# Running every main product of a transformer kernel in 64-row tile mode

## The chip, the cores and the metric

The kernel runs on one core of one Trainium2 chip. The metric is the device time of one execution in microseconds (us), as a median over several executions. Every call on the chip also ran the kernel before, so that each kernel is compared with it on the same chip.

The engines are named as in the profile: PE is TensorE's matmul, PEld its weight load, DVE VectorE, ACT ScalarE, POOL GpSimd, SP SyncE (here it only issues DMAs). PSUM is the memory that PE writes its products to; the program lays it out as eight banks of 128 rows by 512 f32 columns, so that a product of 512 columns takes a whole bank.

## The reference

The reference runs two kinds of layers, A and B, twice each, over 2048 tokens of width 448. Inputs and weights are bf16.

```python
def A(x, wqkv, wo):        # 16 heads of 28; each token sees 8 keys, 2 apart, behind it
    q, k, v = split(x @ wqkv)
    attn = softmax(mask(q . k[s - 2*w]) * 28 ** -0.5)      # w = 0..7
    return (attn . v) @ wo                                  # 448 -> 448
def B(x, w_gate, w_up, w_down):
    return ((x @ w_gate) * (x @ w_up)) @ w_down             # 448 -> 1792 -> 448

x = x + A(layernorm(x)); x = x + B(layernorm(x))
x = x + A(layernorm(x)); x = x + B(layernorm(x))
```

## The kernel before

A small scheduler inside the program takes all operations with their dependences and estimated lengths, and orders them for each engine. It interleaves the attention of one part of the tokens with the feed-forward of another. Some of its settings are the "knobs" of the change: `A_CAP` limits the PSUM banks that attention may hold, `HOLD_A` and `HOLD_BA` say how long an operation of another PE mode waits before it interrupts the main products.

The contraction over 448 is three chunks of 128 rows and one of 64. The program uses PE as one array of 128 rows, or as two tiles of 64 rows that work at the same time (the 64-row mode; in the trace below the two halves start 3 ns apart). The kernel before uses the full array for the 128-row chunks, and pairs the two 64-row remainders of gate and up (or of K and Q, or of two V blocks) in the 64-row mode: six full products and one pair, seven slots in all, for two outputs.

```python
def paired(tag, li, j, first, second, tdeps, prio):
    ...
    first["last"] = full(first, 0, True, ...)       # three 128-row products of gate, mode "F"
    first["last"] = full(first, 1, True)            # three of up, mode "F"
    ...
    tails([(first, False), (second, True)])         # 64-row remainders, both halves at once, mode "R64"
    second["last"] = full(second, 0, False)         # mode "F" again
    second["last"] = full(second, 1, False)

def y_block(li, B, prio):                           # output projection of one block of 128 tokens
    bk = Banks(1)
    ...
    for hc in range(4):
        ins.append((lambda E, hc=hc: E.matmul(ps[:, bk[0], 0:D], oT[:, hc, lo:hi], wo_g[:, hc, :], start=hc == 0, stop=hc == 3), ...))
    sc.add("pe", ins, 4 * pe_cols(D), deps=nd + WO, mode="F", acquire=bk, prio=prio)

# down projection, in b_chunk: 14 full products of 128 rows per block, mode "F"
# gate and up weights: WG and WU [128, 3, F] over all rows, and the remainders in WT [128, F]
```

Attention's own products are in two more modes: scores use tiles of 28 rows ("R32"), values tiles of 32 columns ("C32").

The softmax here doesn't subtract the row's maximum and nothing guards it: scores larger than these inputs give would overflow.

## Time and profile before

| | before |
|---|---|
| median (lowest to highest), 3 runs | 419.69 us (419.61 to 420.73) |
| span of the profiled run | 418.8 us |
| PE busy | 96% of the span |
| DVE, ACT busy | 65%, 50% |
| mean granted clock, profiled run | 0.988 |

The page of the profile gives busy time by engine, busy tenths in 40 slices (PEclk is the granted clock in tenths), and the chain of work that ended last.

```profile
span 418.8 us, 7454 instructions
...
PE 400.5 (96%) x3047; PEld 174.3 (42%) x3092; DVE 273.7 (65%) x553; ACT 210.0 (50%) x341; POOL 28.1 (7%) x40
...
PE   5896999999999999999999999999999999999997
...
PEclk8699999999999999999999999999999999999999
...
PE 88%; DVE 5%; ACT 3%; DMA 2%; issue 1%
```

PE is the limit: after the first tenth of the span it is busy all the time and it makes up most of the chain. The windows of 100 us each say the same (window, length, then busy us of PE, PEld, DVE, ACT and POOL, granted clock, DMA share, GB/s).

```profile
100.00:200.00 100.00, 98.89 (x756) 43.76 (x766) 73.22 (x151) 47.70 (x78) 0.00 (x0) 1.00 0.11 22
200.00:300.00 100.00, 98.73 (x756) 42.79 (x766) 68.58 (x138) 50.38 (x81) 0.00 (x0) 1.00 0.14 25
300.00:400.00 100.00, 98.89 (x665) 41.41 (x672) 57.00 (x105) 42.51 (x70) 0.00 (x0) 1.00 0.10 22
```

"Busy" does not mean "at its peak", because the ends of matmuls are modelled. The groups of the page show it (operation, shapes and count, then busy us, mean ns of one).

```profile
L540 PE MATMUL ps<-xnTb,WU 128*128 128x512 bf16 x330 | 89.8, 379 | 0.8 <-issue 0.3
...
L552 PE MATMUL ps<-xnTb,WT 64*128 64x512 bf16 x224 | 33.8, 381 | 0.0
...
L512 DVE TENSOR_SCALAR xn_sb<-x_sb,mv,rstd 128x512 bf16<-128x512 bf16 x64 | 22.6, 405 | 2.4 <-ACT rstd L506 2.4
```

A product of 512 columns is recorded with 379 ns, but the next one starts after 216. So I read the starts. This is the timeline of PE from 203.8 us (start, length, what, count).

```profile
203.61 0.38 PE L540 MATMUL ps<-xnTb,WG 128*128 128x512 bf16 x1
203.92 0.39 PE L680 MATMUL ps<-qk 28*128 28x120 bf16 x16
204.47 0.59 PE L540 MATMUL ps<-xnTb,WU 128*128 128x512 bf16 x2 [0.16 <-issue]
204.99 0.60 PE L552 MATMUL ps<-xnTb,WT 64*128 64x512 bf16 x4
205.53 0.82 PE L540 MATMUL ps<-xnTb,WG 128*128 128x512 bf16 x3
```

In 2 us the mode changes four times. The single starts of that stretch, in ns, taken from the same trace:

```
204466 full product (128 rows, 512 columns)
204682 full product              + 216   same mode
204994 64-row product, half 1    + 312   mode change: 96 more
204997 64-row product, half 2    +   3   both halves run together
205219 64-row product, half 1    + 222   next pair
205531 full product              + 312   mode change: 96 more than 216
```

DMA issues at the start of the program, as the page lists them (count, KB each, median us from issue to landing):

```profile
WD<-in_B_w_down_dram POOLq DMA_DIRECT2D x1, 1568.0 KB, 14.5
WG<-in_B_w_gate_dram POOLq DMA_DIRECT2D x3, 448.0 KB, 4.7
WU<-in_B_w_up_dram POOLq DMA_DIRECT2D x3, 448.0 KB, 7.9
...
xnTb<-xn_sb SPq DMA_TRANSPOSE x32, 2.5
```

### The profile page before, as it was taken

To read this page: it belongs to the slowest core of one execution; us is meant where nothing else is said; L and a number is where in the kernel's file an instruction comes from. 1 tells how busy PE (TensorE), PEld (TensorE's weight loads), DVE (VectorE), ACT (ScalarE), POOL (GpSimd) and SP (SyncE) were. 2 spreads that over 40 slices of the span, in tenths; PEclk is the share of its full clock that TensorE was granted. 3 is DMA by queue.
4 is the path that set the end of the run, shared out by engine and by line. 5 is a ranking of instruction groups with operands and counts; after the bars stand their busy time and mean duration, and the time that the engine had idled before them with its cause. 6 is when DMAs were issued, how large, how long until landed. Compare 5 with 4: busy or idle time off the path is not lost.

```text
span 418.8 us, 7454 instructions
## 1 busy us (share of the span) xinstructions
PE 400.5 (96%) x3047; PEld 174.3 (42%) x3092; DVE 273.7 (65%) x553; ACT 210.0 (50%) x341; POOL 28.1 (7%) x40
## 2 busy tenths in 40 slices
PE   5896999999999999999999999999999999999997
PEld 3333334444434444444343443434444443444343
DVE  5757897557788647876558875787367846843342
ACT  4579976653456256461555337655255625421320
POOL 3714530000000000000000000000000000000000
PEclk8699999999999999999999999999999999999999
DMA  8793123000003001120100401022100210040001
GB/s 280 224 299 69 37 42 52 13 2 2 13 14 75 2 2 26 26 53 0 27 0 2 77 0 27 2 50 38 34 0 2 50 35 13 0 63 33 0 2 44
DMA packets 37217, 18.08 MB, mean 43 GB/s; under 512 B 31136, under 2 KB 36272, under 8 KB 37184
## 3 DMA queue, kind: packets, MB, share of 16 engines
q1 hardware_dynamic: 34880, 11.02, 12.4%
q0 software_dynamic: 1152, 5.22, 4.1%
q10 hardware_dynamic: 1152, 1.38, 0.9%
q8 instruction: 24, 0.39, 0.4%
q14 instruction: 9, 0.07, 0.1%
HBM read 8.43 MB, written 1.84 MB: 25 GB/s over the span
## 4 chain that ended last, share of the span: by engine, by line
PE 88%; DVE 5%; ACT 3%; DMA 2%; issue 1%
PE ps L540 47%; PE ps L797 20%; PE ps L552 10%; PE ps L742 5%; PE ps L711 2%; PE ps L680 2%; ACT E_sb L687 1%; DVE qk L614 1%; PE ps L579 1%; DMA x_sb<-in_A_x_dram 1%; DVE st L501 1%; DVE oT L728 1%; DMA xnTb<-xn_sb 1%; DVE E_sb L693 1%; DVE x_sb L747 1%
## 5 line engine op out<-in xcount | busy, mean ns | idle before, releaser
L785 DVE TENSOR_TENSOR hT<-g_sb,ps 128x512 bf16<-128x512 bf16 x112 | 74.5, 684 | 32.5 <-ACT g_sb L782 25.2
L782 ACT ACTIVATE g_sb<-ps 128x512 bf16<-128x512 f32 x112 | 64.7, 599 | 58.2 <-PE ps L552 48.2
L540 PE MATMUL ps<-xnTb,WU 128*128 128x512 bf16 x330 | 89.8, 379 | 0.8 <-issue 0.3
L797 PE MATMUL ps<-WD,hT 128*128 128x448 bf16 x448 | 89.4, 353 | 0.0
L540 PE MATMUL ps<-xnTb,WG 128*128 128x512 bf16 x310 | 85.6, 380 | 2.5 <-issue 2.2
L687 ACT ACTIVATE E_sb<-ps 128x960 bf16<-128x960 f32 (+1 forms) x72 | 63.5, 925 | 40.9 <-PE ps L680 40.8
L747 DVE TENSOR_TENSOR x_sb<-x_sb,ps 128x448 bf16<-128x448 bf16 x64 | 39.5, 617 | 42.2 <-PE ps L797 32.6
L693 DVE TENSOR_TENSOR E_sb<-E_sb,MK 128x960 bf16<-128x960 bf16 (+1 forms) x64 | 41.6, 651 | 37.1 <-ACT E_sb L687 36.8
L797 PEld LDWEIGHTS ps<-WD,hT 128*128 128x128 bf16 x448 | 43.0, 98 | 41.0 <-issue 0.4
L540 PE MATMUL ps<-xnTa,WQK 128*128 128x512 bf16 x179 | 46.4, 392 | 3.5 <-ACT WQK L462 1.6
L540 PEld LDWEIGHTS ps<-xnTb,WU 128*128 128x128 bf16 x336 | 32.5, 98 | 38.3
L540 PEld LDWEIGHTS ps<-xnTb,WG 128*128 128x128 bf16 x336 | 27.7, 98 | 48.2 <-issue 24.0
L614 ACT ACTIVATE qk<-ps 128x1024 bf16<-128x1024 f32 x24 | 24.5, 1022 | 42.2 <-PE ps L552 37.1
L501 DVE BATCH_NORM_STATS2 st<-x_sb 128x6 f32<-128x448 bf16 x64 | 39.3, 618 | 4.3 <-DMA x_sb<-in_A_x_dram 3.3
L552 PE MATMUL ps<-xnTb,WT 64*128 64x512 bf16 x224 | 33.8, 381 | 0.0
L742 PE MATMUL ps<-wo_g,oT 128*128 128x448 bf16 x128 | 29.2, 353 | 0.5 <-DVE oT L728 0.4
L540 PEld LDWEIGHTS ps<-xnTa,WQK 128*128 128x128 bf16 x192 | 17.3, 99 | 28.0 <-issue 7.7
L728 DVE TENSOR_TENSOR oT<-ps,R_sb 128x480 bf16<-128x480 f32 (+1 forms) x36 | 22.5, 625 | 8.6 <-ACT R_sb L724 7.9
L660 ACT ACTIVATE v_sb<-ps 128x896 bf16<-128x896 f32 (+1 forms) x13 | 11.4, 888 | 26.2 <-PE ps L552 25.4
L722 ACT ACTIVATE R_sb<-R_sb 128x480 f32<-128x480 f32 (+1 forms) x32 | 18.4, 575 | 11.5 <-DVE R_sb L720 11.5
L512 DVE TENSOR_SCALAR xn_sb<-x_sb,mv,rstd 128x512 bf16<-128x512 bf16 x64 | 22.6, 405 | 2.4 <-ACT rstd L506 2.4
L540 PE MATMUL ps<-WV,xnTa 128*128 128x448 bf16 x96 | 21.0, 353 | 0.8 <-ACT E_sb L687 0.8
(58 smaller groups left out, 230.5 us busy)
## 6 DMA issues: line engine op xcount, KB each, us to landing
x_sb<-in_A_x_dram SPq DMA_DIRECT2D x4, 448.0 KB, 7.8
out_dram<-x_sb SPq DMA_DIRECT2D x16, 112.0 KB, 1.7
WD<-in_B_w_down_dram POOLq DMA_DIRECT2D x1, 1568.0 KB, 14.5
WG<-in_B_w_gate_dram POOLq DMA_DIRECT2D x3, 448.0 KB, 4.7
WU<-in_B_w_up_dram POOLq DMA_DIRECT2D x3, 448.0 KB, 7.9
hT<-in_A_wqkv_dram ACTq DMA_DIRECT2D x4, 224.0 KB, 5.8
xnTb<-xn_sb SPq DMA_TRANSPOSE x32, 2.5
WV<-in_A_wqkv_dram ACTq DMA_DIRECT2D x4, 112.0 KB, 6.4
```

What stands on the lines that cost most here:

```text
L501: sc.add("dve", one(lambda E, B=B: E.bn_stats(st6[:, B, :], x_sb[:, B, :]), ("bn", li, B)), 525.0, deps=[("x", li - 1, B)] + ([("xn", li - ...
L540: ins.append((lambda E, u=u, c=c, st=st, sp_=sp_, which=which: E.matmul(u["out"](which), u["lhs"](which, c, 0, 128), u["rhs"](which, c, 0, ...
L552: ins.append((lambda E, u=u, c=c, lo=lo, which=which, opening=opening: E.matmul(u["out"](which), u["lhs"](which, c, lo, lo + 64), u["rhs"] ...
L614: return E.activation(dst, src, ACT.Copy) if hasattr(E, "activation") else E.tensor_copy(dst, src)
L687: return E.activation(E_sb[0:nk, slot, 2 * hp:2 * hp + 2, 0:4 * nq], ps[0:nk, b0:b0 + 2, 0:4 * nq], ACT.Exp, scale=SCALE)
L693: return E.tensor_tensor(e, e, m, ALU.mult)
L728: return E.tensor_tensor(oT[:, :, tok:tok + nq], ps[:, bk[0], 0:4 * nq].rearrange("p (h n) -> p h n", h=4), R_sb[:, rs, 0:4 * nq].rearrang ...
L742: ins.append((lambda E, hc=hc: E.matmul(ps[:, bk[0], 0:D], oT[:, hc, lo:hi], wo_g[:, hc, :], start=hc == 0, stop=hc == 3), ("Y", li, B) if ...
L747: sc.add("dve", one(lambda E: E.tensor_tensor(x_sb[:, B, :], x_sb[:, B, :], ps[:, bk[0], 0:D], ALU.add), ("x", li, B)), dve_est(D), deps=[ ...
L782: sc.add("act", one(lambda E, gs=gs, bk=bk: E.activation(g_sb[:, gs, :], ps[:, bk[0], :], ACT.Copy), ("G", li, j, fc)), act_est(512), deps ...
L785: sc.add("dve", one(lambda E, gs=gs, bk=bk, fc=fc: E.tensor_tensor(hT[:, fc, hs, :], g_sb[:, gs, :], ps[:, bk[1], :], ALU.mult), ("H", li, ...
L797: ins.append((lambda E, fc=fc, bk=bk, i=i: E.matmul(ps[:, bk[0], 0:D], hT[:, fc, hs, 128 * i:128 * i + 128], WD[:, fc, :], start=fc == 0, ...
```

## The change

The intent is that all main products run in one mode, the 64-row mode, so that PE changes modes only around attention. There are two ways to do it:

- Gate and up: the normalised input is written twice, the copies side by side (896 columns for 448), so that after the DMA transpose the same 64 rows stand on rows 0 to 63 and on rows 64 to 127. The gate weights lie on rows 0 to 63 and the up weights on rows 64 to 127. Each slot is one gate product on one half and one up product on the other; no output ever changes halves.
- Q/K, V, the output projection and the down projection: their inputs are not duplicated. Output 0 takes its products from rows 0 to 63 while output 1 takes those of rows 64 to 127; then the two change places. I call the change of places a cross. There the program makes PE wait on its own semaphore for the first step before the other half writes to the same bank. The scheduler tries to put other products in between (`SELF_LAT`).

The cut core of the diff:

```diff
-TAILS = True
+MAIN = "R64"
...
-HOLD_A = 1000.0
-HOLD_BA = 3000.0
+HOLD_A = 0.0
+HOLD_BA = 1000.0
...
-A_CAP = 4
+A_CAP = 5
...
+    SELF_LAT = 180.0
...
-    xn_sb = sb([128, NXN, 512], bf, "xn_sb")
+    xn_sb = sb([128, NXN, 896], bf, "xn_sb")
-    WG = sb([128, 3, F], bf, "WG")
-    WU = sb([128, 3, F], bf, "WU")
-    WT = sb([128, F], bf, "WT")
+    WGU = sb([128, 7, F], bf, "WGU")
...
+    for q in range(2):
+        fs = slice(896 * q, 896 * q + 896)
+        for nm, lo, src in (("wg", 0, B_w_gate), ("wu", 64, B_w_up)):
+            plain_dma("pool", WGU[lo:lo + 64, :, fs], src.rearrange("(k p) f -> p k f", p=64)[:, :, fs], ...)
...
+                src = _twice_view(x_sb[:, B, :])                 # layer B: every 64 columns twice
+                dst = xn_sb[:, slot, :].rearrange("p (a t n) -> p a t n", a=7, t=2)
...
+    def crossed(parts, deps, prio, est, acquire):                # a part on the other half waits on PE itself
+        ...
+            prev = sc.add("pe", ins, len(ins) / 2 * est, ..., mode=MAIN, ..., after=prev, selfd=prevk if cross else ())
+    def twin(u, tdeps, prio): ...                                # K/Q and V: three slots, cross, four slots
+    def twin_blocks(outs, lhs, rhs, keys, groups, ...): ...      # output and down: two blocks, flip 0, cross, flip 1
...
-            paired("GU", li, j, us[2 * m], us[2 * m + 1], tdeps, prio)
+            for k in range(7):
+                for w in range(2):
+                    ins.append((lambda E, u=u, k=k, w=w: E.matmul(u["out"](w), WGU[64 * w:64 * w + 64, k, ...],
+                                 X[64 * w:64 * w + 64, k, c0:c0 + 512], start=k == 0, stop=k == 6), ...))
```

The rest of the diff is bookkeeping: a smaller `oT` with its own reuse rules, two blocks at a time in the output and down projections, and the removal of the `promise` counter.

## The prediction

> **What bounds it now.** TensorE: busy 96% on the page, 88% of the chain that ended last. In the windows from 100 to 400 us PE is busy 98.7 to 98.9 of each 100 us (DVE 57 to 73, ACT 43 to 50), at clock 1.00. The listed PE waits add up to 14 us, nearly all before 65 us.
>
> Read from the starts of matmul records: full-array products (128 rows) start 216 ns apart for 512 columns, 189 ns for 448. In the 64-row tail mode two start 3 to 4 ns apart, and the next pair 216 ns after, in the seven stretches longer than two pairs. A pair costs what one full product costs: **the change removes no streaming time**.
>
> It removes mode switches. Full to 64-row takes 312 ns start to start instead of 216, back 309, into attention's 28-row or 32-column products 309 to 312, out again some 95 over streaming. I count 260 switches at a median excess of 95 ns (25 us), plus 10 ns in the first slot after each. [...]
>
> **After.** Main products share one mode; only attention's stretches (35 score, 33 value now; at most 72) and a few transposes stand out: 140 to 150 switches. Saved: 110 to 120, so 10.5 to 11.5 us, plus 1 us of first slots, all on the critical path, as PE doesn't idle there.
>
> **What it adds.**
> - Crosses: QK 32, V 20, output projection 16, down 16, together 84; gate/up none. Each waits for PE's own first half. [...] Unfilled, one costs (estimate) 160 ns of drain (376 recorded minus 216), 50 ns (matmul end to the exponential's start) and a 95 ns weight load: 300 ns. Nearly all should be filled by other products of at least 290 ns; I charge 2.5 us.
> - Twice the instructions in main products: four per 216 ns, 54 ns each. The trace sustains 29 ns each over 8 us: issue doesn't bind.
> - Gate/up normalisation writes 896 columns for 512: 405 ns becomes 0.6 us, 32 times, 6 us of DVE. Their DMA transposes take 7 blocks for 4: issue 1.26 us becomes 2.2. Before the first gate/up the chain has four normalisations and 2.4 us of transpose wait, with DVE busy 10 of 10 us. That start slips 4 us; PE fills part; I charge 2 us.
> - End: the last two blocks finish together, one 617 ns add more.
> - Two banks per output and down group; gate and up finish together: tighter PSUM.
>
> **Predicted: 411.5 us, 80% range 405 to 417.** Faster by over 2%: 0.48, within 2%: 0.48, slower: 0.04.
>
> **What would show it.** Pairs 216/189 ns apart through whole gate/up and down stretches; switches near 145; PE idle on its own semaphore below 4 us; PE idle before 70 us up by 1 to 3 us; DVE busy up 6 us; xnTb transposes about 2.2 us; PE still above 97% busy from 100 to 400 us.
>
> **What would make it wrong.** Sustained pairs slower than 216 ns (weight loads of the same rows no longer hidden): 10 ns per slot over about 1600 slots is 16 us. Crosses unfilled: 84 times 300 ns is 25 us. Bank limits opening PE gaps. On the good side, all crosses filled and no slip at the start: 406 us.

The sum: −10.5 to −11.5 us for the switches and −1 for the first slots (−12 in all), +2.5 for the crosses, +2 for the later start and +0.6 for the end come to −6.9 us, which from 419.7 makes 412.8; it wrote 411.5. Of the 300 ns of an unfilled cross all parts are times in the trace of before, though no run shows a drain; that is only the name for the 376 ns of a record less the 216 ns to the next start. The 2.2 us of a transpose are 1.26 us times 7/4; how 405 ns become 0.6 us is not said (in proportion to the columns it would be 0.71).

## The result

| | before | after | after again, later |
|---|---|---|---|
| median | 419.94 us (4 runs) | 415.09 us (4 runs) | 416.03 us (4 runs; before there: 420.00) |
| lowest to highest | 419.61 to 420.73 | 414.31 to 417.02 | 415.31 to 416.73 |
| ratio to before, 95% interval | | 0.9889 (0.985 to 0.9927) | 0.9903 (0.9887 to 0.9918) |
| span of the profiled run | 418.8 us | 412.6 us | 414.1 us |

A ratio is the mean time of one kernel's fast runs over that of the other's of the same rounds, so it is not quite the ratio of the medians. The change made the kernel about 1.0% faster, so it counts as the same within 2%. The profiled run of after happened to be its fastest and that of before one of its slowest, so the two profiles are 6.2 us apart where the medians are 4 to 5 us apart.

The page after:

```profile
span 412.6 us, 10678 instructions
...
PE 394.3 (96%) x4668; PEld 187.3 (45%) x4668; DVE 279.5 (68%) x557; ACT 210.0 (51%) x340; POOL 21.4 (5%) x33
...
PE   5897898899999999999999999999999999999996
...
PEclk9798999999999999999999999999999999999999
...
PE 88%; DVE 6%; ACT 2%; DMA 2%; issue 1%; DVEq 0%; SPq 0%
```

PE still rules, DVE is 5.8 us busier (279.5 for 273.7), and three slices of the head, 5, 7 and 8 (each 10.3 us), are thinner than before. The windows of after:

```profile
100.00:200.00 100.00, 99.40 (x1202) 47.59 (x1200) 72.19 (x148) 52.39 (x84) 0.00 (x0) 1.00 0.17 30
200.00:300.00 100.00, 99.14 (x1248) 47.62 (x1242) 75.21 (x152) 56.46 (x90) 0.00 (x0) 1.00 0.16 31
300.00:400.00 100.00, 100.00 (x1038) 47.43 (x1036) 52.54 (x94) 31.66 (x56) 0.00 (x0) 1.00 0.16 34
```

Twice the main instructions don't hurt PE. The groups that answer to those of before:

```profile
L782 PE MATMUL ps<-xnTb,WGU 64*128 64x512 bf16 x1568 | 177.7, 376 | 2.9 <-ACT g_sb L788 0.9
...
L522 DVE TENSOR_SCALAR xn_sb<-x_sb,mv,rstd 128x512 bf16<-128x512 bf16 (+1 forms) x64 | 33.1, 573 | 1.2 <-ACT rstd L506 0.8
```

The second one mixes two shapes, so I also show it with the shapes kept apart: the doubled write costs 731 ns.

```profile
L522 DVE TENSOR_SCALAR xn_sb<-x_sb,mv,rstd 128x896 bf16<-128x896 bf16 x32 | 21.4, 731 | 0.6 <-ACT rstd L506 0.6
```

The timeline of PE in after shows what is left of the switches: two kinds of attention products, then back to the main mode. In the view's window gate/up pairs then follow each other without a break.

```profile
271.43 0.39 PE L719 MATMUL ps<-E_sb,v_sb 128*32 128x120 bf16 x16
271.75 0.39 PE L688 MATMUL ps<-qk 28*128 28x120 bf16 x16
272.27 1.04 PE L782 MATMUL ps<-xnTb,WGU 64*128 64x512 bf16 x8
```

DMA issues after:

```profile
WGU<-in_B_w_gate_dram POOLq DMA_DIRECT2D x2, 784.0 KB, 10.4
WGU<-in_B_w_up_dram POOLq DMA_DIRECT2D x2, 784.0 KB, 13.5
WD<-in_B_w_down_dram POOLq DMA_DIRECT2D x1, 1568.0 KB, 21.3
...
xnTb<-xn_sb SPq DMA_TRANSPOSE x32, 3.1
```

The same 1568 KB of down weights land 21.3 us after their issue instead of 14.5.

### Where the time went

I split the time of PE by the starts of its matmul records. A slot (one full product, or the 64-row pair, or the four small tiles that start 2 to 5 ns apart) is charged its streaming time, 216 ns for 512 columns and 189 for 448. What is left until the next slot starts is called a switch, up to 110 ns, if the mode changed there; the extra of a half-speed clock, if the granted clock was 0.5 there (products of 512 columns then start 426 to 427 ns apart); "small" up to 14 ns; otherwise a wait, named after the semaphore that PE waited on. Of before, 45 matmul records are missing from the trace (3047 for 3092 weight loads); a gap that fits a missing slot counts as streaming.

| us, profiled runs | before | after | after again |
|---|---|---|---|
| before the first matmul | 1.1 | 1.1 | 1.1 |
| streaming | 368.9 | 369.2 | 369.2 |
| switches (count) | 25.8 (260) | 12.7 (124) | 12.6 (124) |
| small | 2.5 | 1.4 | 1.4 |
| half-speed clock near the start | 4.8 | 5.6 | 5.7 |
| waits | 12.6 | 18.9 | 20.4 |
| – of these, on PE's own semaphore (crosses) | 0 | 2.6 (10) | 2.6 (10) |
| – of these, on ACT or DVE for a bank, after 76 us | 0.3 | 1.8 (10) | 2.0 (11) |
| last matmul start to the end | 3.1 | 3.6 | 3.6 |

From before to after: switches −13.1, small −1.1, waits +6.3, clock +0.9, end +0.5, streaming +0.3, together −6.2, which is the difference of the spans. The change did what it was made for, and waits took back nearly half of it. The experiments ask what a switch and a cross really cost, and what the new waits are.

### The profile page after: what moved, and what is told of

Its sections match the earlier page's. It is cut to its first block, busy times and chain, and to the rows that moved or that the text cites. A ratio compares the mean times of both kernels' runs of the same rounds, so it can differ in the third digit from the quotient of the medians.

```text
span 412.6 us, 10678 instructions
## 1 busy us (share of the span) xinstructions
PE 394.3 (96%) x4668; PEld 187.3 (45%) x4668; DVE 279.5 (68%) x557; ACT 210.0 (51%) x340; POOL 21.4 (5%) x33
## 4 chain that ended last, share of the span: by engine, by line
PE 88%; DVE 6%; ACT 2%; DMA 2%; issue 1%; DVEq 0%; SPq 0%
PE ps L782 39%; PE ps L584 26%; PE ps L568 18%; PE ps L719 2%; PE ps L688 2%; DMA x_sb<-in_A_x_dram 2%; DVE x_sb L756 1%; DVE xn_sb L522 1%; DVE E_sb L701 1%; DVE qk L619 1%; ACT E_sb L695 1%; DVE st L501 1%; DMA xnTa<-xn_sb 1%; DVE oT L739 1%; ACT g_sb L788 1%
## 5 line engine op out<-in xcount | busy, mean ns | idle before, releaser
L782 PE MATMUL ps<-xnTb,WGU 64*128 64x512 bf16 x1568 | 177.7, 376 | 2.9 <-ACT g_sb L788 0.9
L782 PEld LDWEIGHTS ps<-xnTb,WGU 64*128 64x128 bf16 x1568 | 76.7, 94 | 90.8 <-issue 3.0
L584 PE MATMUL ps<-WD,hT 64*128 64x448 bf16 x896 | 90.0, 349 | 0.2
L695 ACT ACTIVATE E_sb<-ps 128x960 bf16<-128x960 f32 (+1 forms) x72 | 64.4, 928 | 18.1 <-PE ps L688 17.4
L584 PEld LDWEIGHTS ps<-WD,hT 64*128 64x128 bf16 x896 | 42.9, 94 | 39.9 <-issue 0.3
L756 DVE TENSOR_TENSOR x_sb<-x_sb,ps 128x448 bf16<-128x448 bf16 x64 | 37.3, 615 | 30.3 <-PE ps L584 29.9
L568 PE MATMUL ps<-xnTa,WQK 64*128 64x512 bf16 x448 | 54.3, 386 | 2.1 <-ACT WQK L459 1.6
L568 PEld LDWEIGHTS ps<-xnTa,WQK 64*128 64x128 bf16 x448 | 21.2, 96 | 29.8 <-issue 2.8
L522 DVE TENSOR_SCALAR xn_sb<-x_sb,mv,rstd 128x512 bf16<-128x512 bf16 (+1 forms) x64 | 33.1, 573 | 1.2 <-ACT rstd L506 0.8
L568 PE MATMUL ps<-WV,xnTa 64*128 64x448 bf16 (+1 forms) x280 | 30.8, 343 | 1.3 <-DVE x_sb L756 0.8
L619 ACT ACTIVATE qk<-ps 128x1024 bf16<-128x1024 f32 x21 | 21.4, 1022 | 19.8 <-PE ps L568 19.7
L584 PE MATMUL ps<-wo_g,oT 64*128 64x448 bf16 x256 | 29.6, 350 | 1.6 <-DVE v_sb L668 0.9
L730 ACT ACTIVATE R_sb<-R_sb 128x480 f32<-128x480 f32 (+1 forms) x32 | 18.5, 577 | 18.9 <-DVE R_sb L728 18.6
L732 ACT ACTIVATE R_sb<-R_sb 128x480 f32<-128x480 f32 (+1 forms) x36 | 21.1, 587 | 0.5
L619 DVE CAST qk<-ps 128x1024 bf16<-128x1024 f32 x11 | 13.4, 1223 | 10.9 <-PE ps L568 10.8
## 6 DMA issues: line engine op xcount, KB each, us to landing
WD<-in_B_w_down_dram POOLq DMA_DIRECT2D x1, 1568.0 KB, 21.3
```

Source lines behind the costliest of these rows:

```text
L522: sc.add("dve", one(lambda E, B=B, dst=dst, src=src: E.tensor_scalar(dst, src, mv[:, B, 0:1], rstd[:, B:B + 1], ALU.subtract, ALU.mult), ( ...
L568: parts[0 if s < 3 else 1][1].append((lambda E, w=w, c=c, lo=lo, st=st, sp_=sp_: E.matmul(u["out"](w), u["lhs"](w, c, lo, lo + 64), u["rhs ...
L584: ins.append((lambda E, w=w, c=c, lo=lo, st=st, sp_=sp_: E.matmul(outs(w), lhs(w, c, lo), rhs(w, c, lo), start=st, stop=sp_), keys[w] if s ...
L619: return E.activation(dst, src, ACT.Copy) if hasattr(E, "activation") else E.tensor_copy(dst, src)
L695: return E.activation(E_sb[0:nk, slot, 2 * hp:2 * hp + 2, 0:4 * nq], ps[0:nk, b0:b0 + 2, 0:4 * nq], ACT.Exp, scale=SCALE)
L756: sc.add("dve", one(lambda E: E.tensor_tensor(x_sb[:, B, :], x_sb[:, B, :], ps[:, bk[w], 0:D], ALU.add), ("x", li, B)), dve_est(D), deps=[ ...
```

## The experiments

Theory: the saved switches are worth 95 ns each; the gain is given back by unfilled crosses, by waits for banks when gate and up finish together, and by a later start of the feed-forward. Rivals: the mode change is not what costs (the gain came from the new order settings); the late start comes not from the wider copy and transposes but from the weight loads; what is taken away in one place is waited for in another.

### After, once more

The kernel is unchanged.

> The changed kernel again, more rounds, beside the next three. Both theories: 414 to 417 us, ratio 0.986 to 0.993. Its profiled span should split as before: switches about 12.7 us against 25.8 in the kernel before, PE waits about 18 us against 12.6.

Measured: 416.03 us, ratio 0.9903 (0.9887 to 0.9918). The account above repeats within 0.1 us in every line but the waits (20.4 for 18.9). Two places make up the difference: the first input landed later (PE's first waits for the normalisation are 0.7 us longer), and one wait near 46 us was 1.69 us instead of 0.85. What follows: the gain is real and near 1%, and the head of the program is what varies. This run is the base of the experiments of its kind below.

### One extra switch in and out of every gate/up unit

Ahead of each unit's first product, a 16-column product in full-array mode goes into the gate bank and is overwritten by the product after it. Results stay right.

```diff
+    if k == 0 and w == 0:
+        def first(E, u=u):
+            E.matmul(u["out"](0)[:, 0:16], warm[:, 0:128], warm[:, 0:16], start=True, stop=True)
+            return E.matmul(u["out"](0), WGU[0:64, 0, ...], X[0:64, 0, c0:c0 + 512], start=True, stop=False)
```

> The changed kernel with one 16-column full-array product ahead of each of the 112 gate/up units, same order of work. It adds up to 224 mode switches. Theory (a switch costs 95 ns of PE time on the path wherever it stands): 112 times about 200 ns, plus 20 to 24 us, so 435 to 439 us. Rival (switches are mostly hidden by waits, and the gain came from the new order of work): plus less than 10 us.

Measured (single run): 438.63 us, 22.6 over the base. The account shows 330 switches for 124 and 33.4 us of switches for 12.6: 206 more switches cost 20.7 us, 100 ns each. 1.1 us more streaming (112 small products) and 1.1 us of small first-slot extras make up the rest; the waits did not grow. So the price of a switch is causal, and the 13.1 us that the account gives for the 136 removed ones stand. What PE does in the about 95 ns of a change was not shown.

### A shorter gate copy

ACT copies only 256 of 512 gate columns; the rest of `g_sb` was set to zero at the start. The result is wrong. (The comparison with the reference passed all the same, so its tolerance is too wide to see half of the gate missing; passing it says little in these experiments.)

```diff
-  E.activation(g_sb[:, gs, :], ps[:, bk[0], :], ACT.Copy)
+  E.activation(g_sb[:, gs, 0:256], ps[:, bk[0], 0:256], ACT.Copy)
```

> The changed kernel with the gate copy on ScalarE cut from 512 to 256 columns, planned order unchanged; the result is wrong on purpose. The copy drops from 0.60 to about 0.38 us. Theory (about a dozen gate/up starts after a score stretch wait some 190 ns each for the gate bank that this copy frees): those waits vanish, and so does the 1 us wait near 73 us; minus 2 to 3 us against the changed kernel of this call. Rival (these waits are the price of a two-semaphore wait or of leaving the score mode, not of the copy): waits stay near 190 ns, time within 0.5 us.

Measured: 414.03 us, ratio 0.9854 (0.9837 to 0.987), 2.0 us less than the base of the same rounds. The copy took 384 ns instead of 597. The waits on ACT and DVE after 76 us fell from 2.04 us (11) to 0.30 us (2), while three waits of V and Q/K products on ACT alone grew by 0.5 us in all. The long wait for the gate copy near 73 us did not vanish as expected; it is in the base and in this run:

```profile
PE ps L782 <- ACT g_sb L788: 0.9, 1, 0.9
```

```profile
PE ps L786 <- ACT g_sb L792: 0.7, 1, 0.7
```

The trace shows how such a wait comes about; these are events of the profiled after, in ns, at the place of the timeline above:

```
271931 PE   last score product (28 rows) starts
272127 ACT  gate copy of an earlier unit ends (it began at 271530): its bank is free
272165 PE   semaphore instruction that waited for ACT starts
272241 PE   weight load of the gate/up unit starts
272272 PE   first gate/up product starts
```

In the kernel before, gate finished three slots ahead of up in every second unit, so that its copy began early. Now both banks finish together in every unit, and while attention's scores hold four banks the next unit has to take a bank whose copy has only just ended. Without the wait, score to main mode takes 143 ns start to start; here it took 341. In the trace the wait for the second semaphore is an instruction of its own, which starts 76 ns ahead of the weight load (272165 and 272241). In after, the product starts 135 to 136 ns after the update of the semaphore that this extra instruction waited for (16 waits), but 44 to 47 ns after the last update where no such instruction ended the wait; so about 90 of the 188 ns of such a bank wait are the price of the extra instruction. What follows: the bank waits are a real cost, 1.7 us in the traces and 2.0 us in the medians. Whether gate and up finishing together is their only cause this run does not show (see the exchanged settings below).

### Light copies for the first feed-forward block

The first layer-B block that is needed gets the old width back: 512 columns normalised and 4 transposed blocks instead of 896 and 7. The missing input rows are zero, so the result is wrong.

```diff
+  light = li == 1 and j == 0
+  dst = xn_sb[:, slot, 0:512]... if light else xn_sb[:, slot, :]...
-  E.dma_start_transpose(X[:, :, c0:c0 + 128], xn_sb[:, slot, 0:128 * nt])
+  E.dma_start_transpose(X[:, 0:nd, c0:c0 + 128], xn_sb[:, slot, 0:128 * nd])      # nd = 4 if light
```

> The changed kernel with the first gate/up chunk alone normalised into 512 instead of 896 columns and transposed in 4 instead of 7 blocks, planned order unchanged; wrong result on purpose. Theory (the wider copies and transposes delay the first gate/up start, 69.1 us now): it starts 1 to 3 us earlier and the PE waits before 76 us shrink by 1 to 2 us, minus 1 to 2 us in all. Rival (that start is set by attention work before it): start within 0.5 us, time the same.

Measured: 415.68 us, ratio 0.9898 (0.9882 to 0.9914), the same as the base (0.9903). The first gate/up product started at 69.9 us, where the two profiles of after have 69.07 and 70.57. PE's wait right before it stayed 0.84 us, and in after it ended with a residual addition of DVE, not with a transpose:

```profile
PE ps L782 <- DVE x_sb L756: 0.8, 1, 0.8
```

So the wider copy and transposes are not what the head pays for, within what this comparison can see (the start lies 0.65 us before that of after again). The prediction's reason for its 2 us was wrong.

### Crosses left unfilled

The scheduler now takes the second step of a cross at once, with nothing in between.

```diff
-    SELF_LAT = 180.0
+    SELF_LAT = 0.0
+                if e == "pe":
+                    best = next((op for op in okay if op.selfd), best)
-            prev = sc.add("pe", ins, len(ins) / 2 * est, ...
+            prev = sc.add("pe", ins, len(ins) / 2 * est + (250.0 if cross else 0.0), ...
```

> The changed kernel with every cross issued straight after its own first half, so that all 84 wait for PE's own semaphore (10 did). Theory (an unfilled cross costs 255 ns, and the filling is what keeps crosses cheap): 74 more times 255 ns, plus 15 to 20 us, so 430 to 435 us. Rival (crosses cost little either way): plus less than 5 us.

Measured (single run): 438.88 us, 22.9 over the base and above the 430 to 435 expected. All 84 crosses now wait: 21.4 us on PE's own semaphore, 255 ns each (start to start 440 ns for 448 columns instead of 189). The 74 newly unfilled ones are 18.8 us of the 22.9. Most of the rest is in the head, where one wait for the attention's input grew:

```profile
PE ps L570 <- DVE x_sb L758: 5.6, 1, 5.6
```

What follows: a cross costs 255 ns when nothing fills it, and shows no wait when it is filled. The scheduler of after fills 74 of 84.

### Output and down projection back in full-array mode

These two drop their 32 crosses and the pairing of blocks (old code for `y_block` and the down loop), and gate/up, Q/K and V stay in 64-row mode.

```diff
-        twin_blocks(lambda w: ps[:, bk[w], 0:D], ..., oT[lo:lo + 64, ...], ... wo_g[lo:lo + 64, c, :], ...)
+        for hc in range(4):
+            ins.append((... E.matmul(ps[:, bk[0], 0:D], oT[:, hc, ...], wo_g[:, hc, :], start=hc == 0, stop=hc == 3) ...))
+        sc.add("pe", ins, 4 * pe_cols(D), deps=nd + WO, mode="F", acquire=bk, prio=prio)
     # the same for hT and WD in the down projection, 14 products per block, two parts
```

> The changed kernel with the attention output and down products back in full-array mode, one bank per block: 32 crosses fewer, about 47 more switches (4.5 us), PSUM looser. Theory (what one saves the other spends): within 3 us of the changed kernel, 413 to 418 us. Rival 1 (switches are all that counts): 419 to 420 us. Rival 2 (crosses and two-bank groups are what ate the gain): under 412 us.

Measured: 417.74 us, ratio 0.9952 (0.9933 to 0.997). It has 171 switches and 17.2 us of them, 4.6 us more than the base; its waits are 2.5 us shorter and its end 0.5 us shorter. So half of the gain can be had with gate/up, Q/K and V alone, and going all the way in one mode is worth about 2 us more: the crosses of the output and down projections don't cost what they save.

### The order settings, exchanged

The kernel before with the new settings, and the kernel after with the old ones:

```diff
 # before                      # after
-HOLD_A = 1000.0              -HOLD_A = 0.0
-HOLD_BA = 3000.0             -HOLD_BA = 1000.0
-A_CAP = 4                    -A_CAP = 5
+HOLD_A = 0.0                 +HOLD_A = 1000.0
+HOLD_BA = 1000.0             +HOLD_BA = 3000.0
+A_CAP = 5                    +A_CAP = 4
```

> The kernel before with the three order settings of the change (attention cap 5 banks, hold times 0 and 1 us). Theory (the gain is from the modes, the settings only fit the new work): slower than before, 421 to 426 us. Rival (the settings are part of the gain): 413 to 418 us.

> The changed kernel with the order settings of the kernel before (attention cap 4 banks, hold times 1 and 3 us). Theory (two-bank groups make PSUM tighter, so a cap of 4 starves attention): slower than the changed kernel by over 8 us, with new PE waits of microseconds, though the switches stay near 130. Rival (PSUM isn't tight): within 3 us of the changed kernel.

Measured: before with the new settings (three rounds) took 428.85 us, ratio 1.0203 (1.0184 to 1.0222), above the 421 to 426 expected. After with the old settings (single run) took 435.42 us, with 10.3 us of waits on DVE, 5.3 us on ACT or DVE and 2.0 us on DMA after 76 us. So the settings are no gain by themselves: each set fits only its own kernel. The rival that the gain came from the settings falls. What the change is worth depends on how well the order around it was tuned: with the old settings in both kernels it costs 15 us (435.42 for 419.97), with the new ones in both it gains 13.

The traces of the last pair say more. Before with the new settings has 270 switches (26.7 us) and 24.4 us of waits and half-speed clock; after again has 124 (12.6 us) and 26.1 us. The spans differ by 13.4 us (427.5 and 414.1), nearly the 14.1 us of the switches. Before with its own settings has 17.4 us of waits and clock. So at the new settings nearly the whole price of the switches is kept, and how much the waits seem to take back depends on the settings that one compares at. For the bank waits too: before with the new settings has 2.8 us of waits on ACT and DVE after 76 us (17, most of it in two of 0.9 and 1.2 us), with its own settings 0.3, although its gate still finishes first in every second unit.

### The up weights from a second queue

The two loads of the up weights are issued by SP, ahead of its transposes, instead of by POOL behind the gate weights. Sizes and places stay.

```diff
+    at = next(i for i, op in enumerate(sc.order["sp"]) if op.dma.startswith("d_t"))
+    for op in [op for op in sc.order["pool"] if op.dma in ("d_wu0", "d_wu1")][::-1]:
+        sc.order["pool"].remove(op)
+        sc.order["sp"].insert(at, op)
+        op.eng = "sp"
```

> The changed kernel with the two up-weight loads (rows 64 to 127) moved from the POOL queue to the SP queue, so that they run beside the gate loads (rows 0 to 63); planned order unchanged. Theory (loads into one 64-row half move at half rate, 84 ns per KB of an engine's packet against 41 in the kernel before; so the down weights land near 37.7 us instead of 33.0, and the transposes that wait for them hold up DVE and then PE): the packets take 41 to 55 ns per KB, the first attention-A transpose starts at 33 to 34.5 us, the PE wait near 46 us (0.9 to 1.8 us) vanishes, minus 0.8 to 2 us against the changed kernel (416.0 in the first call). Rival (the row length of 1792 bytes is slow, not the half): rate and start unchanged, time within 0.5 us.

Background: in the trace of before, a gate or up packet of 7168 bytes, to a load over all 128 rows, took 285 ns (41 ns per KB). In after a packet of 5376 bytes, to a load over 64 rows, took 440 ns (84 ns per KB), and between 18 and 32 us the DMA engines move only 199 to 212 GB/s. The first transposes of the second kind of input wait for the down weights, which come last. In the waits of the SP queue, first before, then after:

```profile
SPq L338 <- DMA WD<-in_B_w_down_dram: 29.7, 1, 29.7
```

```profile
SPq L337 <- DMA WD<-in_B_w_down_dram: 34.5, 1, 34.5
```

Those transposes feed DVE's ring of normalised tiles, then the residual `x_sb`, and then a V product of PE near 46 us. DVE's wait for the ring, first after, then after again:

```profile
DVE xn_sb L522 <- DMA xnTa<-xn_sb: 0.4, 1, 0.4
```

```profile
DVE xn_sb L522 <- DMA xnTa<-xn_sb: 1.2, 1, 1.2
```

PE's waits there, in the same order:

```profile
PE ps L568 <- DVE x_sb L756: 0.8, 1, 0.8
```

```profile
PE ps L568 <- DVE x_sb L756: 1.6, 1, 1.6
```

Measured with two queues: 414.03 us, ratio 0.9855 (0.9838 to 0.9871), about 2 us less than the base. But the rate did not change: 83 to 85 ns per KB, and the two loads ran nearly one after the other, the packets of up from 11.8 to 22.6 us and those of gate from 20.8 to 30.6. The loads started earlier, since SP issued the first at 10.3 us, 3.2 us before POOL's first gate load. The first transposes started at 37.0 us (37.7 and 38.8 in the two profiles of after), not at 33 to 34.5, and the wait near 46 us fell to 0.37 us. Against after again the span is 1.6 us shorter (412.5 for 414.1), 1.3 of it in this wait; against the first after (412.6) it is the same, although the wait there was 0.85 us. Whether the loads of the two halves can run side by side is not shown, as this is no clean test: the gate loads also stood behind the four `wo_g` loads of POOL's queue, which landed only at 17.7 to 23.2 us.

### More room to fill crosses, and two queues

`SELF_LAT` is 250 instead of 180, so that the scheduler keeps more distance in a cross, and V has five buffers instead of four; the two queues stay.

```diff
-    SELF_LAT = 180.0
+    SELF_LAT = 250.0
-    NXN, NV, NE, NR, NG = 6, 4, 3, 3, 4
+    NXN, NV, NE, NR, NG = 6, 5, 3, 3, 4
```

> The same, with the order planned for a cross latency of 250 ns (180 before; 255 measured) and a fifth buffer for V. Theory (unfilled crosses were left because the plan took them for cheaper): fewer than 4 unfilled crosses instead of 10, minus 1 to 3 us against the run before in this call, so 411 to 414 us. Rival (it only moves waits about): within 0.7 us of the run before.

Measured: 414.91 us, ratio 0.9875 (0.9859 to 0.9891), no better than two queues alone (0.9855). The unfilled crosses fell from 10 (2.6 us) to 4 (1.1 us), but the bank waits after 76 us rose from 1.8 us (10) to 3.9 us (15). The rival is nearer here (0.9 us above the run before): the wait moved to another place. That a product that fills a cross holds banks which something else then lacks would explain it; it was not tested.

### Two queues, filled crosses, and other order settings

On top of the last one, eight settings are changed. They were picked by searching over the scheduler's own estimate of the order, not by trials on the chip.

```diff
-HOLD_A = 0.0          +HOLD_A = 1000.0
-HOLD_BA = 1000.0      +HOLD_BA = 0.0
-HOLD_N = 2            +HOLD_N = 3
-DPARTS = ((0, 7), (7, 14))    +DPARTS = ((0, 5), (5, 10), (10, 14))
-POOL_MASK = 2         +POOL_MASK = 1
-LN0 = (1, 1, 2)       +LN0 = (1, 3)
-VFIRST = True         +VFIRST = False
-B_CAP = 8             +B_CAP = 6
```

> The same, with other order settings too (down products in three parts, hold times 1 and 0 us, hold count 3, masks on POOL for the first chunk alone, V after QK at the start). No new theory, a try for the fastest version: 410 to 413 us, faster than the kernel before by 1.6 to 2.4 per cent.

Measured: 410.94 us (410.05 to 411.91), ratio 0.9782 (0.9758 to 0.9805). This is the fastest version: 2.2% under before (1.95 to 2.4, so whether it is over 2% is not settled) and about 1% under after. Its span is 408.3 us; against two queues alone (412.5) the waits before 76 us that are not crosses are 2.4 us shorter (10.8 for 13.2), the half-speed clock 1.8 us, the crosses 1.3 us, while switches (13.1 us) and bank waits (2.6 us) are slightly up. Which of the eight settings does it stays open, and part of it is luck with the throttled clock of the profiled run.

### The same bytes over 128 rows

Gate loads write three chunks and up loads four, each over all 128 rows, with the same 1792 bytes in a piece and the same total. The weights land in wrong places, so the result is wrong. POOL issues them as in after.

```diff
-  plain_dma("pool", WGU[lo:lo + 64, :, fs], src.rearrange("(k p) f -> p k f", p=64)[:, :, fs], ...)
+  k0, nk, step = (0, 3, 128) if nm == "wg" else (3, 4, 106)
+  rows = bass.AP(tensor=src.tensor, offset=src.offset + 896 * q, ap=[[F, 128], [step * F, nk], [1, 896]])
+  plain_dma("pool", WGU[:, k0:k0 + nk, fs], rows, ...)
```

> The changed kernel with the same bytes of gate and up weights, in rows of the same 1792 bytes on the same POOL queue, loaded over 128 rows (3 and 4 row groups a load) instead of into 64-row halves; wrong data on purpose, planned order unchanged. Theory (a load into one half runs at half rate because of the half): the packets drop from 84 to 40 to 50 ns per KB, the rate from 205 to over 300 GB/s, the first attention-A transpose starts at 32.5 to 34.5 us instead of 37.7, the PE wait near 46 us goes, and the time is 1 to 2.5 us below the changed kernel's 415 to 416. Rival (rows of 1792 bytes are the slow part): 80 ns per KB or more, transposes at 37 us or later, time unchanged.

Measured: a packet of 5376 bytes takes 206 ns (gate) to 229 ns (up), 39 to 44 ns per KB, half of after. The rate of the first 80 us in slices of 2 us, first after, then this run:

```profile
GB/s 12 278 391 385 376 164 139 132 253 208 199 208 207 208 202 212 333 308 22 66 118 57 100 105 92 8 0 0 0 0 63 129 161 114 0 8 0 0 0 8
```

```profile
GB/s 8 248 384 387 378 201 68 170 271 398 378 382 356 340 251 16 66 127 70 130 13 0 0 66 66 8 0 0 0 0 22 101 170 174 0 8 0 0 0 0
```

The stretch of 199 to 212 GB/s from 18 to 32 us becomes one of 340 to 398 from 18 to 28 us. The down weights are there 14.2 us after their issue, SP waits for them 28.3 us, the first transposes start at 31.5 us (37.7 and 38.8 in after), and PE's wait near 46 us is short:

```profile
WD<-in_B_w_down_dram POOLq DMA_DIRECT2D x1, 1568.0 KB, 14.2
```

```profile
SPq L337 <- DMA WD<-in_B_w_down_dram: 28.3, 1, 28.3
```

```profile
PE ps L570 <- DVE x_sb L758: 0.3, 1, 0.3
```

So it is the rows that these loads cover, 64 or 128, that set their rate here, 84 against 39 to 44 ns per KB, and not the length of the pieces, 1792 bytes in both. Why the loads into 64 rows are slower was not shown.

What it is worth in time is less sharp. The median is 415.05 us, ratio 0.9858 (0.9837 to 0.9879), which is 0.3 to 0.45 points below after; but in this call the kernel before was slower too (421.2 us), so the microseconds themselves match the first runs of after. The trace is the better witness. In this run and in after again the first input landed equally late (PE's first waits sum to 4.1 and 4.2 us), and the wait near 46 us is 0.38 us for 1.69, the first gate/up product at 69.4 us for 70.6. Against the first after the wait is 0.5 us shorter. So the half-row loads cost between 0.5 and 1.3 us, as far as these waits tell. Transposes that start 6 to 7 us earlier bring no more than that.

## Why the prediction was right or wrong

The predicted time was 411.5 us, with 405 to 417 as its range. The kernel took 415.1 and 416.0 us in two sets of rounds, inside the range but in its upper part; faster and same within 2% were given equal chances, and it was the same. The prediction's own terms sum to −12 + 2.5 + 2 + 0.6 = −6.9, so 412.8 us; the 411.5 that it wrote was lower than its arithmetic.

- **Pairs cost what full products cost** (right). Streaming is 368.9 us before and 369.2 after. Pairs start 216 and 189 ns apart through whole stretches, and in the windows PE is 99.1 to 100% busy. These spacings are sustained: after 76 us the median of 610 gaps between full products of 512 columns in before is 216 ns, the shortest 215, and between pairs in after the medians are 216 and 189 ns, the shortest 215 and 188. Issue and weight loads don't bind: a pair has two weight loads of 94 ns (median) and two products in its 216 ns, each load lies within the 216 ns of a product on the same rows, and the spacing stayed.
- **Switches** (price right, size too small). 140 to 150 were expected, 124 were there; 10.5 to 11.5 us were expected to be saved, it was 13.1. First slots: 1 us expected, 1.1 measured. The extra switches confirm the price (100 ns each).
- **Crosses** (right). 2.5 us charged, 2.6 measured, from ten unfilled crosses at 255 ns, where the estimate had 300.
- **Later start of gate/up** (size of the delay right, reason wrong). It slipped 3.7 us in the first profile of after (65.4 to 69.1) and 5.2 in the other, where 4 were predicted; the agreement is luck. Of the 3.7 us some 1.5 are other products that the new order puts first (44.6 us of streaming before the first gate/up product, about 43 in before) and cost nothing, and 1.8 are seven unfilled crosses; 13 fewer switches take off 1.2, and waits and clock add the rest. The transposes of 7 blocks held the queue for only 1.30 us, not 2.2, and landed after 3.1 us instead of 2.5; giving the first block its old width back left the time as it was. The weight loads into 64 rows at half the rate are shown as one cause, worth 0.5 to 1.3 us, but not as that of the slip: with full-rate loads the start was still at 69.4 us. The waits of the first 76 us without crosses rose by 1.5 us in one profile of after and by 2.8 in the other; what the loads don't explain of it is spread over many small waits, and stays open.
- **Tighter PSUM** (named, but not charged). It was worth about 2 us: ten or eleven waits, nearly all for a gate bank, most of them taken away by the shorter copy. This is the term of the sum that failed by being left out. How much of it belongs to gate and up finishing together and how much to the new settings, which bring such waits to the kernel before too, stays open.
- **Half-speed clock** (not foreseen). 0.9 us more near the start in the profiled run; the granted clock was 0.5 from 7.6 to 17.9 us in before, from 9.0 to 15.8 and from 36.3 to 39.7 us in after. What sets off the throttle was not tested.
- **End** (right): +0.5 us for 0.6. **DVE** (right in sum by luck, off the critical path): its busy time rose by 5.8 us for 6. But the doubled write took 731 ns, not 600, and all normalisation rose by 10.5 us (22.6 to 33.1); the busy time of other groups fell, such as the residual additions from 39.5 to 37.3.

In the medians 4 to 5 us are left of a gross gain of 14.2 us (13.1 and 1.1). The profile of the fastest run accounts for 8.0 us given back: 2.6 in crosses, 1.5 in bank waits, 2.2 in other waits, 0.9 in clock, 0.5 at the end and 0.3 in streaming. This is the account of mode change and settings together. The medians lie 1 to 2 us above that, partly because the profiled run of before was itself 0.6 us above its median, and partly through the head, which varies from run to run (waits of 18.9 and 20.4 us in the two profiles).

## What to carry to other kernels

Count mode changes on PE from the starts of its products, since the busy time hides them (PE was 98.7 to 98.9% busy in the windows of before); each costs about 95 ns here, and keeping one mode paid although it doubles the main instructions. Before splitting an output over row halves, ask what fills the wait of the cross (255 ns here where nothing does), and what finishing two banks at once does to the evacuation: in the account the crosses took back 2.6 us of this gain and the bank waits 1.5, and in the run that filled more crosses the bank waits grew from 1.8 to 3.9 us. The layout that puts each weight on half of the rows also halved the rate at which it was loaded here (84 for 39 to 44 ns per KB), so start such loads earlier, and tune the order again, since the settings of the old kernel cost the new one 19 us (single run). Compare a change at equal settings before you say what took back its gain.
